# Which queue loads which half of the weights, and the order of the preparations in the first units of an FFT and maxout kernel

## The chip, the core and the metric

The kernel runs on one core of one Trainium2 chip. The metric is the device time of one execution in microseconds, the median over several runs. A kernel's profile is taken in an execution of its own and shows the span from its first to its last instruction. The engines are called TensorE (PE; PEld for its weight loads), VectorE (DVE), ScalarE (ACT), GpSimd (POOL) and SyncE (SP). DMAs that POOL issues go over the software queue, those of SP and ACT over hardware queues.

## The reference

For x of shape (8, 3072, 256): the real part of a two-dimensional Fourier transform over sequence and features, seen as 24576 rows of 256, and on it a maxout network with one output layer.

```python
X = np.fft.fft(np.fft.fft(x, axis=1), axis=2).real      # 8 x 3072 x 256
x = X.reshape(24576, 256)
h = np.maximum(np.maximum(x @ w1, x @ w2), x @ w3)      # 24576 x 768
out = h @ w_out                                         # 24576 x 256
```

w1, w2 and w3 are 256 x 768, w_out is 768 x 256, all float32.

## The kernel before

**The arithmetic.** The transform over the sequence is done in two stages, a transform of length 24 (the s steps, `s_half` and `s` in `Mix`) and one of length 128 with a table of sines (the k steps, `Mix.k`, and `Mix.end`). The s steps fill `z` (copied by `s_out`, L566), the k steps fill `t`, with its even part tE and odd part tO (copied by ACT at L610). The transform over the features is not done on x at all: its matrix `md` is multiplied into the weights. Since the maximum of three products is `x @ w1 + max(0, x @ (w2 - w1), x @ (w3 - w1))`, the kernel needs the differences d2 = w2 - w1 and d3 = w3 - w1 (`differences`, L231), then the products of md with them (`prep_first`, L481) and of md, w1 and w_out (`prep_second`, L506).

**The preparations.** `prep_first(jh, bank)` treats one half of the 768 columns (jh is 0 or 1): two pairs of matmuls for d3, two for d2, in four steps. After each step DVE copies the result to `gE` (L495), or ACT to `gO` (L497); `gD`, written by DVE at L501, is the product times the factor `dif`, which is derived from `sgn`. `gE`, `gO` and `gD` are written once per half; index 0 belongs to d2, index 1 to d3. `prep_second` has three g1t steps (md times w1, L513; the copies at L517 go to ACT for the first and to DVE for the other two), then psw (g1t times w_out, twelve matmuls at L523, copied to `gw` at L528) and the step `twice` (L531).

**The units.** The main loop (L938) goes over 8 batches, each of 3 blocks of 512 columns, each of 6 units jc of 128 of the 768 columns: 144 units in all. Unit jc makes four matmuls in two banks (`unit_plus`, L620: t times gE and gO), called plus here; ACT reads one bank with Relu into `stmp` (L640), DVE takes the maximum with the other bank into `hp` (L641). Then come the two matmuls of `unit_minus` with gD for the unit before (minus), and ACT and DVE read the same banks a second time, into `hm`. Each of the two banks of a unit has two buffers, so unit n needs the second reading of unit n - 2. After that `plan` runs what is planned for this unit (L978): in batch 0, units 0 to 9, the remaining preparations, k steps 2 to 5, the last sine tables (`tab_sines`, ACT), and the work of POOL that lays out batch 1's x. Units 0 to 2 use the first half of gE, gO and gD, units 3 to 5 the second.

**The order.** Everything is scheduled by hand: each engine executes its instructions in the order in which the program calls them, and waits for the semaphores of others. Tiles come from pools with a fixed number of buffers. The pool `ps_f` has two banks of PSUM; the k steps, the g1t steps, psw and `twice` take turns in them.

**The start.** POOL first issues twelve loads of batch 0's x (three groups of rows in four parts, L261), then three loads of weights (L268 to L270). SP issues the rest (L271 to L274), held back by a dependence on the first part of the last group of x (`last_part[0]`), and behind them the x rows of batch 1 (L463). A load of a half moves 256 x 384 numbers; w1 is converted to bf16 on the way, w2 and w3 arrive in float32 in `raw_w`. POOL then computes `sgn` and `dif` (L465 to L470), fills a few constants (L471 to L475; the last, `mark`, waits for DVE's copies of x, `laid`), makes the d3 difference of the first half and computes row numbers (`store_rows`, L276). DVE makes the d2 difference of the first half (L826); POOL both of the second half (L827), and issues the load of w_out (L828).

Of the kernel before, what the change touches and what calls it, by code (L numbers as in the profile page):

```python
# [13 lines left out]
ALU = mybir.AluOpType  # L14

ROUND = 12582912.0
AFTER = mybir.DependencyInfo(mybir.DependencyClass.Sync, mybir.DependencyReason.DATA)
# [16 lines left out]
def kernel(  # L34
# [9 lines left out]
    nc = tc.nc  # L44
# [39 lines left out]
    gw = consts.tile([128, 896], BF16, tag="gw")  # L84
    rows_m = consts.tile([128, 12 * B], INT32, tag="rows_m")
    mark = consts.tile([1, 1], FP32, tag="mark")
    two_row = consts.tile([128, 128], BF16, tag="two_row")
# [7 lines left out]
    sgn = consts.tile([128, 1], FP32, tag="sgn")  # L95
    dif = consts.tile([128, 1], FP32, tag="dif")
# [129 lines left out]
    raw_w = [consts.tile([128, 2 * DFF], FP32, name=f"raw_w{i}", tag=f"raw_w{i}") for i in (2, 3)]  # L226
# [4 lines left out]
    def differences(eng, jh, which=(0, 1), after=None):  # L231
        for i in which:
            done = eng.tensor_tensor(out=cols((d2_bf, d3_bf)[i], jh), in0=cols(raw_w[i], jh),  # L233
                                     in1=cols(w1_bf, jh), op=ALU.subtract)
            if after is not None:
                tc.add_manual_dep(done.ins, after.ins.name, AFTER, reason="the two share a port")
        return done

    whole = consts.tile([128, 64], FP32, tag="whole")
    rows_f, pidx, late = whole[:, 0:7 * B], whole[:, 56:57], whole[:, 57:58]  # L240
# [19 lines left out]
    for (r0, r1) in ((0, 40), (40, 84), (84, 112)):  # L260
        last_part = load_rows(nc.gpsimd, x0v[:, r0:r1, :], 0, r0, r1)  # L261

    def load_w(eng, wdst, wsrc, jh):
        return eng.dma_start(
            out=cols(wdst, jh),
            in_=wsrc.rearrange("(fc p) j -> p fc j", fc=2)[:, :, jh * 384:(jh + 1) * 384])

    load_w(nc.gpsimd, w1_bf, moe_w1, 0)  # L268
    load_w(nc.gpsimd, raw_w[1], moe_w3, 0)
    load_w(nc.gpsimd, w1_bf, moe_w1, 1)  # L270
    for (wsrc, wdst, jh) in ((moe_w2, raw_w[0], 0), (moe_w3, raw_w[1], 1),  # L271
                             (moe_w2, raw_w[0], 1)):
        ld = load_w(nc.sync, wdst, wsrc, jh)
        tc.add_manual_dep(ld.ins, last_part[0].ins.name, AFTER, reason="x first")  # L274

    def store_rows():  # L276
        rows_v = rows_f.rearrange("p (b r) -> p b r", r=7)
        iota(rows_v[:, :, 0:5], [[S // 2, B], [-1, 5]], base=S // 2 - 1, cm=-12)
        iota(rows_v[:, :, 5], [[S, B]], base=S - 11, cm=-24)
        iota(rows_v[:, :, 6], [[S, B]], base=S, cm=-24)  # L280
        nc.gpsimd.tensor_scalar(out=late, in0=pidx, scalar1=64.0, scalar2=float(S // 2 - 12),
                                op0=ALU.is_ge, op1=ALU.mult)
        nc.gpsimd.tensor_scalar(out=rows_v[:, :, 6], in0=rows_v[:, :, 6], scalar1=late,
                                scalar2=None, op0=ALU.add)
        iota(rows_v[0:1, :, 6], [[S, B]])
        nc.gpsimd.tensor_copy(rows_m[:, 0:7 * B], rows_f)
# [3 lines left out]
    for (name, value) in (("rnd", ROUND), ("n24", -24.0)):  # L290
# [10 lines left out]
                            op0=ALU.mult, op1=ALU.mult)  # L301
# [5 lines left out]
                                   op0=ALU.add, op1=ALU.subtract)  # L307
# [21 lines left out]
    def tab_sines(r0, r1, parts=(0, 1, 2)):  # L329
        wf = rows_of(r0, r1)  # L330
        wr = wf.rearrange("p (r j) -> p r j", j=128)
        if 0 in parts:
            nc.scalar.activation(out=tabs[:, r0:r1, 0, :], in_=wr, func=AX.Sin, scale=-turn)
        if 1 in parts:
            nc.scalar.activation(out=wf, in_=wf, func=AX.Abs)
        if 2 in parts:
            nc.scalar.activation(out=tabs[:, r0:r1, 1, :], in_=wr, func=AX.Sin, scale=-turn,
                                 bias=half_pi[:, 0:1])
# [5 lines left out]
    for (r0, r1) in ((0, 3), (3, 7)):  # L344
# [7 lines left out]
                            op0=ALU.mult)  # L352
# [8 lines left out]
                            op0=ALU.is_le)  # L361
# [4 lines left out]
                            op0=ALU.mult)  # L366
    nc.vector.tensor_scalar(out=six[:, 1:2], in0=ind24[:, 2:3], scalar1=-6.0, scalar2=None,
                            op0=ALU.mult)
    amp = gen.tile([96, 2], FP32, tag="amp")
    nc.vector.tensor_scalar(out=amp[:, 0:1], in0=ind24[:, 2:3], scalar1=ind24[:, 0:1],  # L370
                            scalar2=0.5, op0=ALU.add, op1=ALU.mult)
    nc.vector.tensor_scalar(out=amp[:, 1:2], in0=ind24[:, 2:3], scalar1=0.5, scalar2=None,
                            op0=ALU.mult)
# [7 lines left out]
    for (c0, c1, by) in ((0, 13, 1), (13, 24, 0), (24, 48, 0)):  # L381
        nc.vector.tensor_scalar(out=v24[:, 48 + c0:48 + c1], in0=v24[:, c0:c1],
                                scalar1=six[:, by:by + 1], scalar2=None, op0=ALU.add)
# [3 lines left out]
    for (m, c, by) in ((m24f, 0, ind24), (m24r, 24, ind24[:, ::-1])):  # L387
        nc.vector.tensor_tensor(
            out=m.rearrange("p (g r) -> p g r", g=4),
# [20 lines left out]
    def turn_rows(copy, r0, n, d0, d1):  # L410
        return reverse(copy, xr0, x0_first[:, r0 * 64:(r0 + n) * 64], r0, n, d0, d1)
# [9 lines left out]
    def bf_rows(r0, n):  # L421
# [19 lines left out]
    nc.vector.scalar_tensor_tensor(out=vm, in0=qm, scalar=-256.0 * ROUND, in1=vm,  # L441
                                   op0=ALU.add, op1=ALU.subtract)
    nc.scalar.activation(out=md[0], in_=vm, func=AX.Sin, scale=float(-2.0 * math.pi / 256.0))
    turn_rows(on_dve, 39, 44, 32, 65)
    lay_rows(on_act, bf_rows(40, 44), 40, 44, 12, 33)
    lay_rows(on_dve, bf_rows(40, 44), 40, 44, 0, 12)
# [15 lines left out]

    for ch in range(4):  # L463
        raw[1, ch] = load_chunk(1, ch)
    nc.gpsimd.tensor_scalar(out=sgn, in0=pidx, scalar1=0.0, scalar2=None,  # L465
                            op0=ALU.is_equal)
    nc.gpsimd.tensor_scalar(out=sgn, in0=sgn, scalar1=2.0, scalar2=-1.0,
                            op0=ALU.mult, op1=ALU.add)
    nc.gpsimd.tensor_scalar(out=dif, in0=sgn, scalar1=1.0, scalar2=None,
                            op0=ALU.subtract)  # L470
    nc.gpsimd.memset(two_row, 0.0)  # L471
    nc.gpsimd.memset(two_row[0:1], 2.0)
    nc.gpsimd.memset(gw[:, 512:513], 0.0)
    nc.gpsimd.memset(gw[0:1, 512:513], 1.0)
    first_op = nc.gpsimd.memset(mark, 0.0)  # L475
    tc.add_manual_dep(first_op.ins, laid.ins.name, AFTER, reason="the two share a port")

# [336 lines left out]
    m = Mix(0)  # L814
# [5 lines left out]
    for k in range(7):  # L820
        m.s_half(k, later, banks_s[k])
        m.s_out(k, banks_s[k], nc.vector.tensor_copy if k % 2 else nc.scalar.copy)
        if k == 1:
            differences(nc.gpsimd, 0, (1,))
            store_rows()
    first_half = differences(nc.vector, 0, (0,))  # L826
    differences(nc.gpsimd, 1, (1, 0), after=first_half)  # L827
    nc.gpsimd.dma_start(out=wout_bf.rearrange("p (jc c) -> p jc c", jc=NJC),  # L828
# [71 lines left out]
            pass  # L900
        l2_odd(0, 0)

    for (u, fn) in ((0, prep_some), (0, prep_some), (0, lambda: tab_sines(7, 10, (2,))),
                    (1, prep_some), (1, prep_some), (1, prep_some),
                    (2, lambda: m.k(2)), (2, prep_some), (2, lambda: tab_sines(10, 13, (0,))),
                    (3, prep_some), (3, lambda: tab_sines(10, 13, (1, 2))),
                    (4, lambda: m.k(3)), (4, prep_some), (5, prep_some), (5, l2_first),
                    (6, lambda: m.k(4)), (7, lambda: m.k(5)), (7, m.end),
                    (0, lambda: turn_chunk(1, 0)), (2, lambda: tab_minus(10, 13, nc.gpsimd)),
                    (2, lambda: turn_chunk(1, 1)),  # L910
                    (5, lambda: turn_chunk(1, 2)),
                    (7, lambda: turn_last(0)), (8, lambda: turn_last(1)),
                    (8, lambda: lay_last(0)), (9, lambda: lay_last(1)), (20, signed)):
        at(0, u, fn)
# [101 lines left out]
```

## Time and profile before

| | us |
|---|---|
| median of 3 runs | 406.31 (405.14 to 406.63) |
| profiled execution | 405.96 |
| its span | 404.1 |
| PE busy in the span | 387.6 |
| DVE busy | 308.2 |
| POOL busy | 298.1 |
| ACT busy | 265.2 |

PE is the busiest engine, with 96% of the span. The chain of work that ended last is PE's own for 92% of the span, DMA's for 4%, POOL's for 2%. Before the first unit lies the start, in which x is loaded, turned and sent through the s steps; PE's first matmuls, at 9.67, only multiply a table (`warm_up`). A timeline row reads: start, length, engine, line and operation, what is written and read, partitions and elements, the count of merged instructions, and in brackets the idle time of the engine ahead of it with what ended it. Matmuls are pipelined: the next one starts before the length given for the one before is over, so their starts, not their lengths, tell how long PE is occupied.

### The profile page before, as it was taken

Reading aid. Unit: us, or ns where it says so; the run is one execution under the profiler, and the core shown is the slowest. Engines: PE = TensorE matmul, PEld = TensorE weight load, DVE = VectorE, ACT = ScalarE, POOL = GpSimd, SP = SyncE. Lnnn points to the kernel's source line nnn. Section 1 sums busy time; section 2 is a strip of 40 time slices with the busy share of each in tenths; the row PEclk is TensorE's granted clock in tenths of the full one; section 3 lists DMA queues with packets and bytes.
Section 4 is the critical chain, followed back from the end, with each engine's and each line's share of the span. In section 5 each row is a group of like instructions: output and inputs, shape, how many; then the busy total and the mean of one; then the engine's idle time right before and its main releaser. Section 6 shows DMA issues by size and latency. Waiting matters only on the chain.

```text
span 404.1 us, 8723 instructions
## 1 busy us (share of the span) xinstructions
PE 387.6 (96%) x2936; PEld 260.0 (64%) x2936; DVE 308.2 (76%) x553; ACT 265.2 (66%) x488; POOL 298.1 (74%) x399
## 2 busy tenths in 40 slices
PE   0889999999999999999999999999999999999996
PEld 0445677766676666666666666766667677666665
DVE  8788776778777876687776887787777877678883
ACT  6878767656767567656776677666766676655550
POOL 9989989879987898679967898768967524323521
PEclk9999999999999999999999999999999999999999
DMA  9979897699878847796579728886234412211214
GB/s 114 185 180 171 172 241 201 162 216 195 190 183 207 192 131 180 198 214 170 131 201 232 163 72 226 213 174 177 74 110 118 118 55 78 80 54 53 106 54 157
DMA packets 127438, 62.08 MB, mean 154 GB/s; under 512 B 111616, under 2 KB 116496, under 8 KB 126816
## 3 DMA queue, kind: packets, MB, share of 16 engines
q1 hardware_dynamic: 101704, 41.82, 41.6%
q0 software_dynamic: 24752, 19.37, 24.5%
q8 instruction: 23, 0.38, 0.4%
q10 hardware_dynamic: 936, 0.33, 0.3%
q14 instruction: 23, 0.19, 0.2%
HBM read 33.74 MB, written 29.88 MB: 157 GB/s over the span
## 4 chain that ended last, share of the span: by engine, by line
PE 92%; DMA 4%; POOL 2%; DVE 1%; issue 0%; ACT 0%; SPq 0%; POOLq 0%; ACTq 0%
PE po L651 31%; PE pse L626 15%; PE pse L634 15%; PE pse L627 15%; PE ps L561 3%; PE po L675 3%; PE ps L608 3%; PE ps L606 3%; PE pl L664 2%; DMA raw_w<-in_moe_w_dram 2%; POOL x L111 2%; DMA x<-in_x_dram 2%; DVE hm L641 1%; POOL d_bf L233 0%; PE psw L523 0%
## 5 line engine op out<-in xcount | busy, mean ns | idle before, releaser
L640 ACT ACTIVATE stmp<-pse 128x512 bf16<-128x512 f32 x288 | 170.8, 600 | 53.6 <-PE pse L627 34.9
L641 DVE TENSOR_TENSOR hp<-pse,stmp 128x512 bf16<-128x512 f32 x144 | 99.6, 691 | 80.8 <-ACT stmp L640 52.9
L681 POOL TENSOR_TENSOR even<-even,other 128x256 f32<-128x256 f32 x92 | 70.3, 765 | 74.0 <-DVE other L678 73.7
L626 PE MATMUL pse<-t,gE 128*128 128x512 bf16 x288 | 109.2, 379 | 0.7 <-DVE gE L495 0.3
L627 PE MATMUL pse<-t,gO 128*128 128x512 bf16 x288 | 109.0, 378 | 0.0
L641 DVE TENSOR_TENSOR hm<-pse,stmp 128x512 bf16<-128x512 f32 x144 | 99.2, 689 | 3.4 <-ACT stmp L640 3.1
L651 PE MATMUL po<-wout_bf,hp 128*128 128x256 bf16 x576 | 85.9, 272 | 0.0
L634 PE MATMUL pse<-t,gD 128*128 128x512 bf16 x288 | 85.6, 379 | 0.0
L651 PE MATMUL po<-wout_bf,hm 128*128 128x256 bf16 x570 | 85.3, 273 | 0.0
L712 POOL DMA_INDIRECT out_dram<-ot,rows_m x53 | 54.1, 1021 | 20.5 <-DVE ot L705 12.5
L651 PEld LDWEIGHTS <-hp 128*128 128x128 bf16 x576 | 56.3, 98 | 17.3 <-issue 2.5
L651 PEld LDWEIGHTS <-hm 128*128 128x128 bf16 x576 | 56.3, 98 | 16.6
L705 DVE TENSOR_TENSOR ot<-po,even 128x512 f32<-128x512 f32 x92 | 62.8, 682 | 0.0
L173 POOL CAST xw<-xs 96x544 bf16<-96x544 f32 (+1 forms) x48 | 53.4, 1123 | 0.0
L178 POOL CAST xb<-xs 96x512 bf16<-96x512 f32 x48 | 52.5, 1101 | 0.0
L610 ACT CAST t<-ps 128x512 bf16<-128x512 f32 x48 | 27.9, 586 | 34.9 <-PE ps L608 34.8
L634 PEld LDWEIGHTS <-gD 128*128 128x128 bf16 x288 | 28.1, 98 | 32.3
L678 DVE SCALAR_TENSOR_TENSOR other<-twice,po 128x256 f32<-128x256 f32 x92 | 43.8, 476 | 0.1
L627 PEld LDWEIGHTS <-gO 128*128 128x128 bf16 x288 | 28.1, 98 | 20.3 <-issue 2.0
L626 PEld LDWEIGHTS <-gE 128*128 128x128 bf16 x288 | 28.2, 98 | 20.0 <-DVE gE L495 0.7
L570 ACT CAST z_all<-ps 128x480 bf16<-128x480 f32 x45 | 24.2, 561 | 21.6 <-PE ps L561 20.5
L667 ACT COPY even<-pl 128x512 f32<-128x512 f32 x46 | 27.0, 588 | 9.5 <-PE pl L664 8.1
(178 smaller groups left out, 373.9 us busy)
## 6 DMA issues: line engine op xcount, KB each, us to landing
xs<-in_x_dram SPq DMA_DIRECT2D x84, 198.0 KB
out_dram<-ot SPq DMA_DIRECT2D x39, 256.0 KB
xs<-in_x_dram SPq DMA_DIRECT2D x28, 192.0 KB
held<-xb SPq DMA_DIRECT2D x48, 96.0 KB
xw<-held POOLq DMA_DIRECT2D x24, 192.0 KB
out_dram<-ot SPq DMA_DIRECT2D x12, 128.0 KB
raw_w<-in_moe_w_dram SPq DMA_DIRECT2D x3, 384.0 KB
out_dram<-ot,rows_m POOLq DMA_INDIRECT x53
```

The costliest lines, as they stand in the source:

```text
L173: nc.gpsimd.tensor_copy(v[:, d0:d1, ch * 32:ch * 32 + 32], xs[:, 0:32 * 64].rearrange("p (bb dl) -> p dl bb", dl=64)[:, d0:d1, :])
L178: nc.gpsimd.tensor_copy(mir[:, d0:d1, c0:c0 + 32], bass.AP(xs.tensor, xs.offset + 33 * 64 - 1 - d0, [xs.ap[0], [-1, d1 - d0], [-64, 32]]))
L626: nc.tensor.matmul(pse[:, 0:n], gE[i][:, js], te, start=True, stop=False)
L627: nc.tensor.matmul(pse[:, 0:n], gO[i][:, js], to, start=False, stop=True)
L634: nc.tensor.matmul(pse, gD[i][:, js], to, start=False, stop=True, skip_group_check=True)
L640: nc.scalar.activation(out=stmp[:, 0:n], in_=pses[0][:, 0:n], func=AX.Relu)
L641: nc.vector.tensor_tensor(out=dst, in0=src3, in1=stmp[:, 0:n], op=ALU.max)
L651: nc.tensor.matmul(po, hcols(jc), wout_bf[:, jc * 256:(jc + 1) * 256], start=False, stop=(jc == NJC - 1), skip_group_check=True)
L678: nc.vector.scalar_tensor_tensor(out=other, in0=twice, scalar=po[:, 256:257], in1=po[:, 0:256], op0=ALU.mult, op1=ALU.subtract)
L681: nc.gpsimd.tensor_tensor(out=line[:, 256:512], in0=line[:, 0:256], in1=other, op=ALU.add)
L705: nc.vector.tensor_tensor(out=parts, in0=po.rearrange("p (i c) -> p i c", i=2), in1=lin.rearrange("p (i c) -> p i c", i=2), op=ALU.add)
L712: stored(nc.gpsimd.indirect_dma_start(out.rearrange("(n two) c -> n (two c)", two=2) if pair else out, bass.IndirectOffsetOnAxis(ap=rows_m ...
```

## The change

Three things are changed.

The loads: the first half of w2 goes over to POOL's queue, ahead of w1's second half. SP keeps the second halves of w3 and w2, and now waits for the last part of x (`last_part[3]`).

`sgn` and `dif` are computed on DVE, behind the preparation of `md`, no longer on POOL. The four memsets of `two_row` and of the last column of `gw` move on POOL from before the d3 difference of the first half to behind `store_rows`.

The plan of units 0 to 5: k step 2 goes from unit 2 to unit 0; the four steps of `prep_first(1)` go from units 0, 0, 1, 1 to units 1, 1, 2, 2; the three g1t steps from units 1, 2, 3 to units 3, 3, 4; in unit 4 there are now the third g1t step, k step 3 and psw, in this order. `twice` stays in unit 5.

```diff
     load_w(nc.gpsimd, w1_bf, moe_w1, 0)
     load_w(nc.gpsimd, raw_w[1], moe_w3, 0)
+    load_w(nc.gpsimd, raw_w[0], moe_w2, 0)
     load_w(nc.gpsimd, w1_bf, moe_w1, 1)
-    for (wsrc, wdst, jh) in ((moe_w2, raw_w[0], 0), (moe_w3, raw_w[1], 1),
-                             (moe_w2, raw_w[0], 1)):
-        ld = load_w(nc.sync, wdst, wsrc, jh)
-        tc.add_manual_dep(ld.ins, last_part[0].ins.name, AFTER, reason="x first")
+    for (wsrc, wdst) in ((moe_w3, raw_w[1]), (moe_w2, raw_w[0])):
+        ld = load_w(nc.sync, wdst, wsrc, 1)
+        tc.add_manual_dep(ld.ins, last_part[3].ins.name, AFTER, reason="x first")
...
     nc.scalar.activation(out=md[0], in_=vm, func=AX.Sin, scale=float(-2.0 * math.pi / 256.0))
+    nc.vector.tensor_scalar(out=sgn, in0=pidx, scalar1=0.0, scalar2=None,
+                            op0=ALU.is_equal)
+    nc.vector.tensor_scalar(out=sgn, in0=sgn, scalar1=2.0, scalar2=-1.0,
+                            op0=ALU.mult, op1=ALU.add)
+    nc.vector.tensor_scalar(out=dif, in0=sgn, scalar1=1.0, scalar2=None,
+                            op0=ALU.subtract)
     turn_rows(on_dve, 39, 44, 32, 65)
...
-    nc.gpsimd.tensor_scalar(out=sgn, in0=pidx, scalar1=0.0, scalar2=None,
-                            op0=ALU.is_equal)
-    nc.gpsimd.tensor_scalar(out=sgn, in0=sgn, scalar1=2.0, scalar2=-1.0,
-                            op0=ALU.mult, op1=ALU.add)
-    nc.gpsimd.tensor_scalar(out=dif, in0=sgn, scalar1=1.0, scalar2=None,
-                            op0=ALU.subtract)
-    nc.gpsimd.memset(two_row, 0.0)
-    nc.gpsimd.memset(two_row[0:1], 2.0)
-    nc.gpsimd.memset(gw[:, 512:513], 0.0)
-    nc.gpsimd.memset(gw[0:1, 512:513], 1.0)
     first_op = nc.gpsimd.memset(mark, 0.0)
...
             store_rows()
+            nc.gpsimd.memset(two_row, 0.0)
+            nc.gpsimd.memset(two_row[0:1], 2.0)
+            nc.gpsimd.memset(gw[:, 512:513], 0.0)
+            nc.gpsimd.memset(gw[0:1, 512:513], 1.0)
...
-    for (u, fn) in ((0, prep_some), (0, prep_some), (0, lambda: tab_sines(7, 10, (2,))),
-                    (1, prep_some), (1, prep_some), (1, prep_some),
-                    (2, lambda: m.k(2)), (2, prep_some), (2, lambda: tab_sines(10, 13, (0,))),
-                    (3, prep_some), (3, lambda: tab_sines(10, 13, (1, 2))),
-                    (4, lambda: m.k(3)), (4, prep_some), (5, prep_some), (5, l2_first),
+    for (u, fn) in ((0, lambda: tab_sines(7, 10, (2,))), (0, lambda: m.k(2)),
+                    (1, prep_some), (1, prep_some), (2, prep_some), (2, prep_some),
+                    (2, lambda: tab_sines(10, 13, (0,))),
+                    (3, prep_some), (3, prep_some), (3, lambda: tab_sines(10, 13, (1, 2))),
+                    (4, prep_some), (4, lambda: m.k(3)), (4, prep_some),
+                    (5, prep_some), (5, l2_first),
```

## The prediction

> **What bounds the kernel now.** I read the split by stretches first, then the timelines of the first 40 us engine by engine. In the stretches the columns after the length are busy us (and instructions) of PE, PEld, DVE, ACT and POOL, then the granted clock, DMA share and GB/s.
> ```profile
> span 404.1 us, 8723 instructions
> ...
> 21.00:40.00 19.00, 17.28 (x100) 9.69 (x99) 15.39 (x27) 14.39 (x30) 17.56 (x19) 1.00 0.84 170
> 40.00:396.00 356.00, 355.85 (x2644) 240.78 (x2643) 273.45 (x463) 234.91 (x433) 261.18 (x351) 1.00 0.60 152
> ```
> From 40 to 396 us PE is busy 355.85 of 356.00, so whatever moves the first units moves the end one for one. The change touches only what lies before 40. There PE waits, and the rows of POOL and SP say for what (start, length, in brackets the idle time before):
> ```profile
> 13.85 0.76 POOL L264 DMA_DIRECT2D raw_w<-in_moe_w_dram  x1
> 15.02 0.71 POOL L264 DMA_DIRECT2D w_bf<-in_moe_w_dram  x1 [0.41 <-DMA x<-in_x_dram]
> 15.76 1.11 POOL L465 TENSOR_SCALAR sgn<-whole 128x1 f32<-128x1 f32 x1
> ...
> 18.23 0.20 POOL L471 MEMSET two_row<- 128x128 bf16 x1
> ...
> 19.16 1.64 POOL L233 TENSOR_TENSOR d_bf<-raw_w,w_bf 128x768 bf16<-128x768 f32 x1
> ...
> 22.26 1.02 POOL L286 CAST rows_m<-whole 128x56 int32<-128x56 f32 x1
> 24.21 3.24 POOL L233 TENSOR_TENSOR d_bf<-raw_w,w_bf 128x768 bf16<-128x768 f32 x2 [0.93 <-DMA raw_w<-in_moe_w_dram]
> 27.39 0.94 POOL L828 DMA_DIRECT2D wout_bf<-in_moe_w_out_dram  x1
> ...
> 32.66 2.05 POOL L158 CAST x<-xs 96x1056 bf16<-96x1056 f32 x1
> ```
> ```profile
> 15.78 1.44 SPq L264 DMA_DIRECT2D raw_w<-in_moe_w_dram  x3
> 17.26 25.16 SPq L111 DMA_DIRECT2D xs<-in_x_dram  x16
> ```
> The second halves of the weights let POOL begin only at 24.21. On DVE the first half of w2 is late as well, by 0.56 at 22.23:
> ```profile
> 15.32 1.52 DVE L144 COPY back<-x 96x1452 bf16<-96x1452 bf16 x1 [0.85 <-DMA x<-in_x_dram]
> ...
> 18.15 0.70 DVE L417 COPY nat<-x 96x588 bf16<-96x588 bf16 x1
> 19.88 1.79 DVE L570 CAST z_all<-ps 128x480 bf16<-128x480 f32 x3 [1.03 <-PE ps L588]
> 22.23 0.96 DVE L233 TENSOR_TENSOR d_bf<-raw_w,w_bf 128x768 bf16<-128x768 f32 x1 [0.56 <-DMA raw_w<-in_moe_w_dram]
> ...
> 28.87 0.68 DVE L641 TENSOR_TENSOR hm<-pse,stmp 128x512 bf16<-128x512 f32 x1
> 29.47 0.55 DVE L495 CAST gE<-psg 128x384 bf16<-128x384 f32 x1
> 29.93 0.61 DVE L501 TENSOR_SCALAR gD<-psg,dif 128x384 bf16<-128x384 f32 x1
> ...
> 31.69 0.68 DVE L517 CAST g1t<-pst 128x512 bf16<-128x512 f32 x1
> ```
> PE's own rows are the yardstick: the first matmul of units 0 to 5 stands at 24.40, 26.55, 28.93, 31.34, 33.32 and 36.65.
> ```profile
> 24.40 0.39 PE L626 MATMUL pse<-t,gE 128*128 128x512 bf16 x1 [0.33 <-DVE gE L495]
> ...
> 25.06 0.38 PE L627 MATMUL pse<-t,gO 128*128 128x512 bf16 x1
> 25.90 0.81 PE L490 MATMUL psg<-d_bf,md_all 128*128 128x384 bf16 x4 [0.47 <-POOL d_bf L233]
> 26.55 0.38 PE L626 MATMUL pse<-t,gE 128*128 128x512 bf16 x1
> ...
> 28.93 0.38 PE L626 MATMUL pse<-t,gE 128*128 128x512 bf16 x1
> ...
> 29.60 0.38 PE L626 MATMUL pse<-t,gE 128*128 128x512 bf16 x1
> ...
> 31.34 0.38 PE L626 MATMUL pse<-t,gE 128*128 128x512 bf16 x1
> ...
> 33.32 0.38 PE L626 MATMUL pse<-t,gE 128*128 128x512 bf16 x1
> ...
> 34.04 0.38 PE L626 MATMUL pse<-t,gE 128*128 128x512 bf16 x1
> ...
> 35.34 1.47 PE L523 MATMUL psw<-wout_bf,g1t 128*128 128x256 bf16 x12
> 36.65 0.38 PE L626 MATMUL pse<-t,gE 128*128 128x512 bf16 x1
> ```
> Starts lie 0.22 apart for 512 columns (three steps from 24.40 to 25.06), 0.163 for 384 (four from 25.90 to 26.55), 0.11 for 256 (twelve from 35.34 to 36.65). What exceeds this between 24.40 and 36.65 is PE waiting: 0.62 before 25.90, 0.24 before 29.60, 0.24 from 31.34 to 33.32 (six steps of 512 and four of 256 fill 1.74 of it), 0.29 before 34.04: 1.39 in all.
>
> **The change, part by part.**
>
> *First halves.* That of w2 leaves SP's queue for POOL's, where it is issued at 15.02, in the place of w1's second half. The nearest price is w3's first half, issued on the same queue at 13.85 and in use at 19.16: at most 5.3 us. So w2 lands by about 20.3 (estimate); the other bound is its present landing, just before 22.23. DVE is held by its z copies until 19.88 + 1.79 = 21.67 in either case. I take 20.3, since the issue stands on the same queue 1.2 us behind: DVE starts 0.56 earlier, and so does unit 0, at 23.84.
>
> *Second halves.* w1's is issued about 15.8 instead of 15.02. SP's two loads now wait for the last part of x, not for the first of its group; that part is in use on ACT at 17.12, so the wait of 15.78 becomes at most 17.1.
> ```profile
> 17.12 0.80 ACT L144 COPY back<-x 96x261 bf16<-96x261 bf16 x2
> ```
> Behind it on SP stand the second batch's x rows (17.26); POOL first reads them at 32.66, and one load fewer is ahead of them: no cost. For the weights themselves there are two loads to move on SP instead of three, 1.3 us later. POOL can take them only at about 24.1 anyway: its rows last to 23.28, and the four memsets moved behind them add about 0.85 (18.23 to 19.09 now). I take 24.1, next to today's 24.21. PE asks for the result only at 26.5 (below), and POOL gives it at 24.1 + 1.64 = 25.74; a landing after 24.9 would cost us for us. wout's load follows at 27.3, not 27.39, and psw, which needs it, comes later than now: no cost.
>
> *sgn and dif on DVE.* Three 128x1 operations; DVE is idle for 0.85 before 15.32, and that wait for x hides them. Without it they cost at most that idle time. On POOL their going could start the difference of 19.16 up to 0.2 earlier, since DVE's copies, which it waits for, end at 18.85. PE can't use that: k step 0 behind it waits for z at 21.67.
>
> *The other order.* This is the large term. ACT's pieces, each of which starts about 0.1 before the one ahead has ended (two stmp in 1.07):
> ```profile
> 27.13 0.62 ACT L337 ACTIVATE tab<-w_late,half_pi 128x384 bf16<-128x384 f32 x1
> 27.64 1.07 ACT L640 ACTIVATE stmp<-pse 128x512 bf16<-128x512 f32 x2
> ...
> 31.10 0.59 ACT L610 CAST t<-ps 128x512 bf16<-128x512 f32 x1
> ```
> Unit 0 runs from 23.84 to 24.71. k step 2 (0.44) fills the hole in which PE waited for POOL, and unit 1 starts at 25.15, 1.40 ahead of 26.55. Minus 0 waits 0.07 for DVE, the d3 pair runs from 26.5, PE is free at 27.16.
> Unit 2 needs ACT to have read unit 0's sums a second time. ACT now has the sines (0.62) and the t copy (0.59) before that: stmp at 24.91, sines 25.41, t 25.94, stmp 26.44, stmp 26.93 to 27.53. PE starts at 27.57 (0.41 lost), and unit 2's second half waits for DVE's hm of unit 0, done at 28.37: 28.41 (0.41 lost).
> The d2 pair comes after minus 1, from 29.27 to 29.92. Unit 3 needs gE from it. DVE works in order: gE and gD of d3 (0.55, 0.61), hp of unit 2, then hm of unit 1, whose stmp can start only after minus 1 (29.27 to 29.87). So hm runs from 29.92 to 30.61 and gE ends at 31.08. Unit 3 starts at 31.12: 1.19 lost. Today that copy stands at 29.47, a unit before its use.
> Unit 3, minus 2 and two g1t steps (0.88) bring unit 4 to 33.30, level with 33.32. It loses 0.06; minus 3, the third g1t step and k step 3 end at 35.53, and psw stands directly behind both. In the built program psw has the bank that k step 3 used, so it waits for ACT's t copy, which comes after two stmp: 35.74 to 36.33, psw at 36.37 (0.84 lost). Its fifth matmul reads the third g1t, which DVE copies behind hp 4 and hm 3: 37.18 (0.41 lost). Eight more matmuls: unit 5 at 38.10.
> Waiting is now 0.07 + 0.41 + 0.41 + 1.19 + 0.06 + 0.84 + 0.41 = 3.39 against 1.39: +2.00. With unit 0 earlier by 0.56: **+1.44 us**, a span of 405.5. The profiled execution took 405.96 with its span of 404.1, which is 0.35 under the median of the runs, 406.31; added to that median: **407.7**.
>
> A rule speaks against moving w2 to POOL. POOL's issues of x take (min/median/max, ns):
> ```profile
> L111 POOL DMA_DIRECT2D x<-in_x_dram x12: 777/930/1746, 1.5 to 12.3; - x12
> ```
> The Trainium skill, SBUF — State Buffer, section "SBUF: two separate sides", says that GpSimd can't write a DMA's descriptors while VectorE runs certain copies, and that a hardware queue is free of this. The 1746 would fit it; the issue at 15.02, beside DVE's copy of 15.32, took 0.71 and doesn't. By the row the sum is the one above, by the rule the far end of the next case.
>
> **Rivals.** *Late weights (slower).* The place is DVE's difference of w2; it decides once w2 lands after 21.57, and from there each us costs one. If the software queue brings it no sooner than SP's does now, so that the change doesn't do what it says, DVE starts at 22.23 again and +2.00 is left: 408.3. If DVE's copies, which end at 18.85, hold POOL's issue until then, w2 lands at 18.85 + 5.3 = 24.15, DVE starts 2.0 later than now: +4.0, 410.3. For: the 1746. Against: 0.71 at 15.02.
> *The new waits are covered.* The losses at unit 3 and psw rest on the order within DVE and ACT. If they sum to no more than today's 1.39, only -0.56 is left: 405.8. For: DVE is busy 15.39 and ACT 14.39 of 19.00 us. Against: the queues run in order, so idle time elsewhere is no help.
> *All waits go.* Then the 1.39 fall away too: -1.95, 404.4. Only unit 1's early start speaks for it.
>
> **How the numbers follow.** Forecast 0.57 (own range 407.0 to 408.5), late weights 0.25 (408.3 to 410.3; 0.07 of it the held issue), covered waits 0.13 (405.2 to 406.5), all gone 0.05 (403.9 to 404.8). The range leaves out the top of the late weights, the bottom of the covered waits and the last: 405.6 to 409.4. 0.5% of 406.31, about what a measurement of this kernel can tell from no change, is 2.03, so the bounds are 404.28 and 408.34. Faster: over half of the last case, 0.03. Slower: 0.08 of the forecast and 0.23 of the late weights, 0.31. Same: 0.66.
>
> **What would show it.** Right: DVE's difference of w2 at about 21.7 without a wait for its load; unit 1 over 1 us earlier than 26.55; PE idle for about 1.2 us before unit 3, put down to gE on DVE; psw interrupted after four matmuls; unit 5 near 38.1; 40 to 396 as full as now. Wrong: unit 5 at or before 36.65, DVE waiting for raw_w beyond 22.2, or POOL's second differences after 24.9.

## The result and the profile after

The changed kernel is slower by about 0.4%: the ratio to the kernel before is 1.0044, 95% interval 1.0027 to 1.0061, over 17 runs of each. On the median before in this series, 405.26 us, that is +1.78 us (1.09 to 2.47). The median after is 406.81, 1.55 above it. The forecast was +1.44. Its 407.7 lies higher than the measured time because it was put on the first three runs of before, whose median of 406.31 is 1.05 above that of the seventeen.

The head of the page after and its split by stretches (columns as before: busy us and instructions of PE, PEld, DVE, ACT and POOL, granted clock, DMA share, GB/s):

```profile
span 404.6 us, 8724 instructions
...
21.00:40.00 19.00, 16.27 (x93) 8.98 (x93) 13.86 (x24) 13.17 (x27) 17.99 (x20) 1.00 0.80 161
40.00:396.00 356.00, 355.80 (x2640) 240.62 (x2640) 273.23 (x464) 235.31 (x435) 259.79 (x350) 1.00 0.60 152
```

From 40 us on PE is as full as it was: 355.80 of 356.00 against 355.85. Between 21 and 40 PE is busy for 16.27 us instead of 17.28. PE's timeline after, from the last matmul of the s steps to the first of unit 5:

```profile
19.84 0.21 PE L584 MATMUL ps<-m24r,back 96*64 96x96 bf16 x1
...
23.11 0.39 PE L622 MATMUL pse<-t,gE 128*128 128x512 bf16 x1 [0.33 <-DVE gE L491]
...
24.43 0.38 PE L622 MATMUL pse<-t,gE 128*128 128x512 bf16 x1
...
26.94 0.38 PE L622 MATMUL pse<-t,gE 128*128 128x512 bf16 x1 [0.21 <-ACT stmp L636]
...
27.77 0.38 PE L622 MATMUL pse<-t,gE 128*128 128x512 bf16 x1 [0.24 <-DVE hm L637]
...
30.46 0.39 PE L622 MATMUL pse<-t,gE 128*128 128x512 bf16 x1 [1.01 <-DVE gE L491]
...
32.64 0.38 PE L622 MATMUL pse<-t,gE 128*128 128x512 bf16 x1
...
33.34 0.38 PE L622 MATMUL pse<-t,gE 128*128 128x512 bf16 x1
...
35.91 1.64 PE L519 MATMUL psw<-wout_bf,g1t 128*128 128x256 bf16 x12 [0.67 <-ACT t L606]
37.40 0.38 PE L622 MATMUL pse<-t,gE 128*128 128x512 bf16 x1
```

In the profiled execution of before, the same last matmul of the s steps stands 0.74 later:

```profile
20.58 0.21 PE L588 MATMUL ps<-m24r,back 96*64 96x96 bf16 x1
```

So the two executions are compared from that point on. From it to unit 0 it is 3.27 us now and 3.82 before; from unit 0 to unit 5 14.29 and 12.25; from unit 5 to the end of the span 367.20 and 367.45. With -0.74 these make -0.74 - 0.55 + 2.04 - 0.25 = +0.50, the difference of the spans. The work that PE does between unit 0 and unit 5 is the same in both, 12.25 - 1.39 = 10.86, so PE now waits 3.43 us there instead of 1.39. The s steps' end differs by 0.74 between these two executions, so the runs, and not the two spans, tell what the change costs.

### The profile page after: what moved, and what is told of

It is laid out like the page before. It is cut to its first block, busy times and chain, and to the rows that moved or that the text cites. A ratio compares the mean times of both kernels' runs of the same rounds, so it can differ in the third digit from the quotient of the medians.

```text
span 404.6 us, 8724 instructions
## 1 busy us (share of the span) xinstructions
PE 387.7 (96%) x2936; PEld 259.8 (64%) x2936; DVE 308.1 (76%) x556; ACT 264.5 (65%) x488; POOL 295.7 (73%) x397
## 4 chain that ended last, share of the span: by engine, by line
PE 89%; POOL 4%; DMA 3%; ACT 1%; issue 1%; DVE 1%; SPq 0%; POOLq 0%; ACTq 0%
PE po L647 30%; PE pse L622 15%; PE pse L630 15%; PE pse L623 15%; PE po L671 3%; PE ps L557 3%; POOL x L111 3%; PE ps L604 2%; PE ps L602 2%; PE pl L660 2%; DMA raw_w<-in_moe_w_dram 2%; DMA x<-in_x_dram 1%; DVE hm L637 1%; PE psw L519 0%; POOL d_bf L233 0%
```

## The experiments

All were measured against the kernel before in runs of the same chip; a ratio is the time over that of before, with its 95% interval. "Unit 0 to 5" is read from PE's timeline of each run's profile, as above. Short diffs are against the changed kernel unless said otherwise.

**The loads alone.** The changed kernel with the plan of before.

```diff
-    for (u, fn) in ((0, lambda: tab_sines(7, 10, (2,))), (0, lambda: m.k(2)),
-                    (1, prep_some), (1, prep_some), (2, prep_some), (2, prep_some),
...
+    for (u, fn) in ((0, prep_some), (0, prep_some), (0, lambda: tab_sines(7, 10, (2,))),
+                    (1, prep_some), (1, prep_some), (1, prep_some),
...
```

> All of the change but the order: loads, sgn and dif on DVE and the moved memsets as in the changed kernel, units 0 to 4 in the order of before. Theory (the new order costs +2.00, the loads gain 0.56 at unit 0): DVE takes w2's difference straight behind its z copies; PE then waits about 0.8 us instead of 0.62 before the d3 pair of the second halves, because POOL's difference ends at about the same place as now while PE comes earlier; unit 0 to unit 5 takes about 12.4 us (12.25 before, 14.29 in the changed kernel), and the time is 0.4 us below before, ratio 0.999. Rival (the loads are what costs, by later second halves): unit 0 to unit 5 takes over 13.5 us, ratio 1.003 to 1.005.

Ratio 1.0013 (0.9993 to 1.0032): no difference that can be told, and the theory's 0.999 lies outside. Unit 0 to 5 took 35.89 - 23.15 = 12.74, nearer to the theory's 12.4 than to the rival's 13.5, but 0.49 more than in before. PE's rows and one of ACT:

```profile
23.15 0.82 PE L622 MATMUL pse<-t,gE 128*128 128x512 bf16 x2 [0.33 <-DVE gE L491]
24.85 0.81 PE L486 MATMUL psg<-d_bf,md_all 128*128 128x384 bf16 x4 [0.66 <-POOL d_bf L233]
...
32.44 0.38 PE L622 MATMUL pse<-t,gE 128*128 128x512 bf16 x1 [0.23 <-ACT stmp L636]
33.28 0.38 PE L622 MATMUL pse<-t,gE 128*128 128x512 bf16 x1 [0.24 <-DVE hm L637]
...
35.89 0.38 PE L622 MATMUL pse<-t,gE 128*128 128x512 bf16 x1
```

```profile
30.90 0.52 ACT L333 ACTIVATE tab<-w_late 128x384 bf16<-128x384 f32 x1 [0.27 <-POOL w_late L327]
```

Unit 0 came 3.28 after the s steps, 0.54 earlier than in before, and nearly all of that is waited for again: for POOL's difference of the second half before 24.85 (0.82 by the distance of starts, 0.62 in before), and at unit 4, where ACT's reading stands behind sines that wait for POOL's angles.

**The order alone.** The kernel before with the new plan.

> Only the order of units 0 to 4, with the loads, sgn, dif and memsets of before. Theory: unit 0 starts as in before, with the 0.5 us wait of DVE for w2; unit 0 to unit 5 takes 14.2 to 14.3 us against 12.25, PE waits about 1.1 us before unit 3 for gE on DVE, and about 0.8 us before psw for ACT's t copy; ratio 1.005, 0.5 us above the changed kernel. Rival (the order is neutral, the loads cost): 12.3 us, ratio within 1.001 of before.

Ratio 1.0051 (1.0036 to 1.0067). Unit 5's first record is missing in this trace; its second matmul stands at 38.12, so that it began about 0.22 earlier, at 37.90, 14.28 after unit 0. PE's rows:

```profile
23.62 0.82 PE L626 MATMUL pse<-t,gE 128*128 128x512 bf16 x2 [0.33 <-DVE gE L495]
...
30.97 0.39 PE L626 MATMUL pse<-t,gE 128*128 128x512 bf16 x1 [1.01 <-DVE gE L495]
...
36.20 0.60 PE L523 MATMUL psw<-wout_bf,g1t 128*128 128x256 bf16 x4 [0.67 <-ACT t L610]
37.02 1.05 PE L523 MATMUL psw<-wout_bf,g1t 128*128 128x256 bf16 x8 [0.22 <-DVE g1t L517]
```

The order makes the whole loss. The sum of the waits is that of the changed kernel to 0.01 us; only its parts differ, 0.05 at unit 4's second half and 0.38 before psw's fifth matmul here, 0.27 and 0.17 there. DVE's wait for w2, with the old loads, was smaller here than in before's profile, 0.21 instead of 0.56 (DVE's row):

```profile
21.46 0.96 DVE L233 TENSOR_TENSOR d_bf<-raw_w,w_bf 128x768 bf16<-128x768 f32 x1 [0.21 <-DMA raw_w<-in_moe_w_dram]
```

**w2's first half back on SP's queue.**

```diff
-    load_w(nc.gpsimd, raw_w[0], moe_w2, 0)
...
-    for (wsrc, wdst) in ((moe_w3, raw_w[1]), (moe_w2, raw_w[0])):
-        ld = load_w(nc.sync, wdst, wsrc, 1)
+    for (wsrc, wdst, jh) in ((moe_w2, raw_w[0], 0), (moe_w3, raw_w[1], 1),
+                             (moe_w2, raw_w[0], 1)):
+        ld = load_w(nc.sync, wdst, wsrc, jh)
```

> The changed kernel with w2's first half back on SP's queue, ahead of the two second halves, all three behind the last part of x. Theory: w2 lands 1 to 2 us later than in the changed kernel, DVE's difference waits for it by 0.5 us or more, and the whole delay stays: unit 0 and unit 5 are later by the same 0.5 to 1.0 us, ratio 1.0055 to 1.007 to before. Rival (a chain that doesn't begin with w2, through POOL's angles, ACT and the third g1t, sets psw): unit 0 is later, unit 5 is not, ratio 1.0045 as the changed kernel.

Unit 0 to 5 took 15.69 us in the trace (unit 5's first record is missing here and in the next trace too, and its start is reckoned as above). The ratio, 1.0051 (1.0033 to 1.0070), can't be told from the changed kernel's 1.0044. Both theories missed the place. The rows of DVE and of POOL: DVE did not wait for w2 at all, and unit 0 came 3.28 after the s steps, as in the changed kernel; POOL waited for the loads behind w2 on SP.

```profile
20.95 0.95 DVE L233 TENSOR_TENSOR d_bf<-raw_w,w_bf 128x768 bf16<-128x768 f32 x1
```

```profile
25.17 3.25 POOL L233 TENSOR_TENSOR d_bf<-raw_w,w_bf 128x768 bf16<-128x768 f32 x2 [1.97 <-DMA raw_w<-in_moe_w_dram]
```

POOL's lateness went on, through its angles and ACT's sines, to 1.12 us of idle time at unit 4. In the changed kernel the first of these two differences starts 2 us earlier, without a wait; but in the next run, which has the loads of the changed kernel, it waits as well (one row of each):

```profile
23.12 1.65 POOL L233 TENSOR_TENSOR d_bf<-raw_w,w_bf 128x768 bf16<-128x768 f32 x1
```

```profile
24.68 3.24 POOL L233 TENSOR_TENSOR d_bf<-raw_w,w_bf 128x768 bf16<-128x768 f32 x2 [1.23 <-DMA raw_w<-in_moe_w_dram]
```

So this pair of profiles doesn't show that w2's leaving SP is what brings w3's second half early. It does show an execution in which DVE had no wait for w2 that the move could have saved.

**The d2 pair one unit earlier**, straight behind the d3 pair.

```diff
-                    (1, prep_some), (1, prep_some), (2, prep_some), (2, prep_some),
+                    (1, prep_some), (1, prep_some), (1, prep_some), (1, prep_some),
```

> The changed kernel with the d2 pair of the second halves moved up from unit 2 to unit 1, straight behind the d3 pair. Theory: the 1.01 us before unit 3 (gE on DVE) goes to under 0.3, but not for nothing: the d2 pair comes to PE at about 26.5, where POOL's difference of w2 ends at 26.8 and DVE has not yet emptied the two banks of the d3 pair, so that unit 2 starts 0.5 to 2 us later than now; unit 5 is no earlier, 0 to 0.8 us later, ratio 1.004 to 1.0065. Rival (the place of the pair alone makes the wait): unit 3 and unit 5 come 1.0 earlier, ratio 1.002.

Ratio 1.0059 (1.0044 to 1.0075), unit 0 to 5 15.11. As the theory had it, the wait moved: the pair itself now waits for DVE to empty the d3 pair's banks, and unit 3 waits less. Part of it has a second reason: POOL's difference for the pair, the second of the two in this run's row above, ended only at 27.92. PE's rows:

```profile
28.61 1.00 PE L486 MATMUL psg<-d_bf,md_all 128*128 128x384 bf16 x4 [1.42 <-DVE gE L491]
...
31.38 0.38 PE L622 MATMUL pse<-t,gE 128*128 128x512 bf16 x1 [0.47 <-ACT stmp L636]
```

**The third g1t step in unit 3**, so that unit 4 has k step 3 and psw alone.

```diff
-                    (3, prep_some), (3, prep_some), (3, lambda: tab_sines(10, 13, (1, 2))),
-                    (4, prep_some), (4, lambda: m.k(3)), (4, prep_some),
+                    (3, prep_some), (3, prep_some), (3, prep_some), (3, lambda: tab_sines(10, 13, (1, 2))),
+                    (4, lambda: m.k(3)), (4, prep_some),
```

> The changed kernel with the third g1t step moved from unit 4 up to unit 3, so that unit 4 holds k step 3 and psw alone. Theory (psw waits because k step 3 and the third g1t stand right ahead of it): its waits of 0.84 and 0.16 us go, a new one of about 0.4 before the third g1t step (its bank waits for ACT's copy of the first) comes in; unit 0 to unit 5 takes 13.6 us instead of 14.29, ratio 1.0025 to 1.003. Rival (the delay at unit 3 comes through to psw by another chain): psw still waits about 1 us, 14.2 to 14.3 us, ratio 1.0044.

Ratio 1.0013 (0.9999 to 1.0027), unit 0 to 5 13.41: the largest gain of one edit, and the theory's place. The waits of 0.84 and 0.17 are gone. psw starts at 35.23, 0.12 behind the last matmul of k step 3, before ACT can have copied that step, so it no longer has the same bank. The new wait of 0.40 is there, ahead of the third g1t step. PE's rows:

```profile
33.06 0.60 PE L509 MATMUL pst<-md_all,w_bf 128*128 128x256 bf16 x4 [0.24 <-ACT g1t L513]
...
35.23 1.49 PE L519 MATMUL psw<-wout_bf,g1t 128*128 128x256 bf16 x12
36.55 0.38 PE L622 MATMUL pse<-t,gE 128*128 128x512 bf16 x1
```

**One copy of gE moved from DVE to ACT**, the one for which unit 3 waits.

```diff
-                    nc.vector.tensor_copy(out=gE[i][:, cs], in_=psg[:, 0:384])
+                    (nc.vector.tensor_copy if i or not jh else nc.scalar.copy)(
+                        out=gE[i][:, cs], in_=psg[:, 0:384])
```

> The changed kernel with one copy moved from DVE to ACT: gE of the d2 pair's second half, for which PE waits 1.18 us before unit 3. Theory (DVE's order, hp of unit 2 and hm of unit 1 ahead of that copy, makes the wait): the wait falls to about 0.1, 0.4 come back at gO, which now stands behind gE on ACT; unit 3 is 0.7 us earlier, and if the waits add up unit 5 as well: 13.6 us from unit 0, ratio 1.0027. Rival (waits do not add up, what is gained at unit 3 is waited at psw): unit 3 0.7 earlier, unit 5 within 0.2 of the changed kernel, ratio 1.004.

Unit 3 comes 6.58 after unit 0 instead of 7.35, unit 5 13.68 instead of 14.29: DVE's order is the cause of that wait, and 0.61 of the 0.77 comes through in the trace, as the theory had it. The wait before unit 3 goes from 1.18 to 0.41, not to 0.1. PE's row:

```profile
31.54 0.39 PE L623 MATMUL pse<-t,gE 128*128 128x512 bf16 x1 [0.25 <-ACT gE L491]
```

The interval of the ratio, 1.0039 (1.0024 to 1.0054), is too wide to tell the two theories apart.

**The sines of rows 7 to 9 from unit 0 to unit 3.**

```diff
-    for (u, fn) in ((0, lambda: tab_sines(7, 10, (2,))), (0, lambda: m.k(2)),
+    for (u, fn) in ((0, lambda: m.k(2)),
...
-                    (3, prep_some), (3, prep_some), (3, lambda: tab_sines(10, 13, (1, 2))),
+                    (3, prep_some), (3, prep_some), (3, lambda: tab_sines(7, 10, (2,))), (3, lambda: tab_sines(10, 13, (1, 2))),
```

> The changed kernel with the sines of rows 7 to 9 (0.62 us of ACT) moved from unit 0 to unit 3. Theory that the terms add up: the first wait of unit 2 (0.37 us, ACT behind the sines) goes, units 2 to 4 and unit 5 are 0.4 us earlier, ratio 1.0035. Rival (psw is the end of a chain on ACT, and the sines only change their place on it): units 2 to 4 are 0.4 earlier, psw waits 0.3 to 0.5 longer for the t copy, unit 5 stays within 0.1 of 14.29 us after unit 0, ratio 1.0044.

The trace fits the rival; the ratio, 1.0043 (1.0028 to 1.0058), can't tell its 1.0044 from the theory's 1.0035. In this execution the granted clock was low ahead of unit 0 (more of that in the last section); from unit 0 on the starts of the matmuls lie 0.22 apart as elsewhere. Unit 2 comes 0.39 and unit 4 0.51 earlier after unit 0 (3.44 and 9.02 against 3.83 and 9.53), and unit 5 stays at 14.29 to the hundredth, because psw waits 1.20 for the t copy and 0.52 for the third g1t. That last copy starts 12.67 after unit 0, as in the changed kernel (35.78 there): the moved sines stand on ACT ahead of unit 4's stmp, for which DVE waits. PE's rows and one of DVE:

```profile
26.95 0.39 PE L622 MATMUL pse<-t,gE 128*128 128x512 bf16 x1 [0.29 <-DVE gE L491]
...
35.97 0.38 PE L622 MATMUL pse<-t,gE 128*128 128x512 bf16 x1
...
39.39 0.60 PE L519 MATMUL psw<-wout_bf,g1t 128*128 128x256 bf16 x4 [1.03 <-ACT t L606]
40.35 1.05 PE L519 MATMUL psw<-wout_bf,g1t 128*128 128x256 bf16 x8 [0.37 <-DVE g1t L513]
41.24 0.38 PE L622 MATMUL pse<-t,gE 128*128 128x512 bf16 x1
```

```profile
39.62 0.68 DVE L513 CAST g1t<-pst 128x512 bf16<-128x512 f32 x1
```

**Five attempts at a faster version.** They use these findings: the order of before with k step 3 in unit 3 and the last sines in unit 4. The texts put down before these runs call the s steps layer 1.

```diff
+    for (u, fn) in ((0, prep_some), (0, lambda: tab_sines(7, 10, (2,))), (0, prep_some),
+                    (1, prep_some), (1, prep_some), (1, prep_some),
+                    (2, lambda: m.k(2)), (2, prep_some), (2, lambda: tab_sines(10, 13, (0,))),
+                    (3, prep_some), (3, lambda: m.k(3)),
+                    (4, prep_some), (4, lambda: tab_sines(10, 13, (1, 2))),
+                    (5, prep_some), (5, l2_first),
```

The first also computes POOL's last angles on DVE, in its idle time before the z copies, and puts the memsets back in front.

```diff
+    tab_angles(10, 13)
     warm_up(1, third_turned)
...
-    tab_angles(10, 13, nc.gpsimd)
```

> A version put together from what the first runs show: the loads of the changed kernel, the four memsets back where they stood before, the angles of rows 10 to 12 on DVE (two operations of 0.56 us in its 1.06 us of waiting for PE ahead of the z copies) instead of POOL (3.0 us), and the order of before with k step 3 moved from unit 4 to unit 3 and the last sines to unit 4. Theory: POOL's second difference ends 0.7 us earlier than in the run with the loads alone, the 0.82 us before the d3 pair falls to under 0.2, ACT no longer waits for POOL's angles; unit 0 to unit 5 takes 11.3 to 11.8 us (12.25 in before, 12.74 with the loads alone), ratio 0.997 to 0.9985. Rival (the angles delay DVE's z copies, or the second halves land too late): over 12.3 us, ratio 0.9995 or more.

Ratio 0.9990 (0.9977 to 1.0003), unit 0 to 5 11.38, the shortest of all. The trace is where the theory had it; the ratio, outside the theory's range, has an interval that holds the theory's 0.9985 and the rival's 0.9995 alike. Unit 0 comes 3.52 after the s steps, 0.25 later than in the changed kernel. POOL's rows show by what: a memset takes up to 0.79 beside DVE's copies, and the first difference 1.97 instead of 1.65, ending at 21.12.

```profile
17.27 0.79 POOL L472 MEMSET two_row<- 1x128 bf16 x1
...
19.15 1.97 POOL L233 TENSOR_TENSOR d_bf<-raw_w,w_bf 128x768 bf16<-128x768 f32 x1 [0.42 <-DMA raw_w<-in_moe_w_dram]
```

The second has the four memsets behind w_out's load; the third adds k step 2 behind unit 0, with the first g1t step and the sines of rows 7 to 9 one unit later.

> The version of the last run with the four memsets neither in front (where they took 0.55 to 0.79 us each beside DVE's copies and held POOL's first difference to 21.1) nor between POOL's differences, but behind wout's load. Theory: POOL's first difference ends early enough that PE waits under 0.3 us for it instead of 0.74, so that unit 0 comes 3.3 us after the end of layer 1 instead of 3.52; unit 0 to unit 5 stays at 11.2 to 11.7 us; ratio 0.997 to 0.998. Rival (what unit 0 gains is waited for the second halves behind it, whose loads have not landed): unit 0 to unit 5 grows by the same, ratio 0.999.

> The same with k step 2 right behind unit 0, as the changed kernel has it, and the sines of rows 7 to 9 in unit 1. Theory (in the change it is not k step 2 that costs, but the d2 pair a unit later and k step 3 with the third g1t right ahead of psw): k step 2 fills PE's wait before the d3 pair, unit 0 to unit 5 is within 0.3 of the run without this step, 11.2 to 11.8 us, ratio 0.997 to 0.9985. Rival (k step 2's t copy on ACT pushes the stmp of unit 0 back and with it units 2 and 3): over 12.2 us, ratio 1.000 or more.

Ratios 1.0007 (0.9991 to 1.0022) and 0.9999 (0.9986 to 1.0011): no gain. Unit 0 to 5 took 11.39 and 11.62, so in this order k step 2 right behind unit 0 costs little, and it is not what costs in the change; but unit 0 came 4.45 and 4.57 after the s steps. The rows of DVE and of POOL in the version with the late memsets show why: POOL's difference now starts ahead of it, and DVE's second operation of the angles takes 1.89 instead of 0.56, with the z copies behind it.

```profile
18.77 1.89 DVE L322 SCALAR_TENSOR_TENSOR w_late<-w_late 128x384 f32<-128x384 f32 x1
20.59 1.77 DVE L566 CAST z_all<-ps 128x480 bf16<-128x480 f32 x3
```

```profile
18.60 1.65 POOL L233 TENSOR_TENSOR d_bf<-raw_w,w_bf 128x768 bf16<-128x768 f32 x1 [0.17 <-DMA raw_w<-in_moe_w_dram]
```

The fourth is the kernel before with the angles on DVE and this order; the fifth has the new loads, the angles on POOL, the memsets behind them, and w_out's load between POOL's two last differences.

> The loads, sgn, dif and memsets of before, with the angles of rows 10 to 12 on DVE and the order of the last two versions but one (k step 3 in unit 3, the last sines in unit 4). Theory (the change's loads bring the time about nothing, the order and the angles bring what is gained): unit 0 to unit 5 takes 11.3 to 12.0 us, ratio 0.997 to 0.9995, within 0.001 of the version with the new loads. Rival (the new loads gain 0.5 us or more at unit 0): ratio over 0.9995 and at least 0.0015 above the version with the new loads.

> The loads of the changed kernel with POOL's work in another order (no memsets ahead of the second differences but behind the angles, wout's load between the two differences), the angles of rows 10 to 12 on POOL again, and the order of before with k step 3 in unit 3 and the last sines in unit 4. Theory (the 1.9 us of the angles' second operation on DVE beside POOL's difference was the whole of the 1.56 us that PE waited before k step 0): DVE's z copies start without that delay, unit 0 comes 3.3 us after the end of layer 1, the second halves are waited for by 0.3 to 0.5 us twice, unit 0 to unit 5 takes 11.4 to 11.8 us; ratio 0.996 to 0.9985. Rival (an earlier unit 0 only waits longer for the second halves or for wout): unit 0 to unit 5 over 12.2 us, ratio 0.9995 or more.

The old loads gave 1.0008 (0.9992 to 1.0024) with 11.42 us from unit 0 to 5. That is level with the second version, of the same series, and 0.0018 above the first, of another series, more than the rival's 0.0015; the intervals overlap. So what the new loads are worth can't be told here either. The last gave 1.0008 (0.9984 to 1.0033) with 12.36 us: the rival's outcome. Unit 0 was back at 3.27 after the s steps, and PE waited 0.81 and 0.60 by the distance of starts for POOL's differences of the second halves. PE's rows:

```profile
25.21 0.81 PE L486 MATMUL psg<-d_bf,md_all 128*128 128x384 bf16 x4 [0.65 <-POOL d_bf L233]
...
27.75 0.81 PE L486 MATMUL psg<-d_bf,md_all 128*128 128x384 bf16 x4 [0.44 <-POOL d_bf L233]
```

In some of these executions the gain is given back later too. The rows of POOL and of PE in the run with the third g1t in unit 3: POOL waited for the second chunk of batch 1's x, and PE for a bank that DVE could empty only behind POOL.

```profile
39.00 2.01 POOL L158 CAST x<-xs 96x1056 bf16<-96x1056 f32 x1 [1.98 <-DMA xs<-in_x_dram]
```

```profile
49.09 0.27 PE L671 MATMUL po<-gw,t 128*128 128x257 bf16 x1 [0.91 <-DVE ot L701]
```

No version beats the kernel before by more than the measurement can tell.

## Why the prediction was right, point by point

The table sets the places that the prediction gave against the profile after; 0.74 is taken off, since the s steps ended that much earlier there than in the profile on which it was built.

| PE reaches | predicted, less 0.74 | measured |
|---|---|---|
| unit 0 | 23.10 | 23.11 |
| unit 1 | 24.41 | 24.43 |
| unit 2, its second half | 26.83, 27.67 | 26.94, 27.77 |
| unit 3 | 30.38 | 30.46 |
| unit 4 | 32.56 | 32.64 |
| psw | 35.63 | 35.91 |
| unit 5 | 37.36 | 37.40 |

From the last matmul of the s steps to unit 5 the trace after is 2.04 - 0.55 = 1.49 longer than before, where the forecast had 1.44.

*The order* was the large term, as forecast: 3.39 us of waiting predicted, 3.43 measured, with the causes that were named (unit 3 behind gE, psw behind ACT's t copy). The order alone and the loads alone split the change: 14.28 and 12.74 us, ratios 1.0051 and 1.0013. They don't add: the 0.49 that unit 0 to 5 grew by with the loads alone is not in the changed kernel's 14.29, where k step 2 fills the hole ahead of the d3 pair.

*Unit 3's wait* was put down to gE's place on DVE. DVE after:

```profile
28.63 0.68 DVE L637 TENSOR_TENSOR hp<-pse,stmp 128x512 bf16<-128x512 f32 x1
29.24 0.69 DVE L637 TENSOR_TENSOR hm<-pse,stmp 128x512 bf16<-128x512 f32 x1
29.85 0.55 DVE L491 CAST gE<-psg 128x384 bf16<-128x384 f32 x1
...
35.78 0.68 DVE L513 CAST g1t<-pst 128x512 bf16<-128x512 f32 x1
```

hp and hm stand ahead of it, as worked out; with the copy on ACT unit 3 came 0.77 earlier.

*psw's two waits* were sized 0.84 and 0.41. The first is 0.84; of the second only 0.17 is left (35.91 to 37.40 is 1.49 for 1.32 of work), because unit 4's second half had already lost 0.27 instead of 0.06. The fifth matmul can't start before the third g1t copy ends at 36.46, whatever was lost ahead of it. So the 0.84, though it is there, is not a price of its own: without it psw would have begun at 35.08 and stopped before its fifth matmul at 35.52, until the same 36.46 (an estimate from these rows; no run takes the t copy's wait away alone).

*The sum* of the waits came out because each was worked out with those ahead of it already in their places. Its terms are not prices that can be saved one by one. With gE's copy on ACT, 0.61 of the 0.77 saved at unit 3 came through to unit 5. With the late sines, nothing of the 0.39 to 0.51 saved at units 2 to 4 did, because ACT's queue got the same sines back ahead of psw: ACT's t copy and DVE's third g1t are ends of chains that run beside PE.

*w2's first half, -0.56.* Unit 0 came 0.55 earlier after the s steps than in the profile of before, but that this meets the forecast is in part luck. The term was sized from one execution. DVE's wait for w2 with the old loads was 0.56 in one profile and 0.21 in another; with w2 on SP behind the last part of x it was nil, and unit 0 stood at 3.28 all the same. The loads alone bring no time that can be told, and the interval of the result, 1.09 to 2.47, holds the order's +2.00 by itself as well as +1.44: the runs don't confirm this term. The second halves were taken to cost nothing, and in the profile of the changed kernel PE did not wait for them; but POOL waited for the first of them 0.93 in before, 1.97 with w2 on SP and 1.23 with the d2 pair early, and in the other profiles for no load at that place. What decides that is open.

*The rivals.* Late weights did not come: DVE's difference of w2 started at 20.84 without a wait, and unit 0 stands at 3.27 after the s steps. The waits were not covered. Of the 1.39 the 0.62 ahead of the d3 pair did go, as forecast, but the new ones are far larger.

*sgn and dif* took three operations of 0.15 on DVE, from 13.97 to 14.49, and the copy of x followed at 14.52 without a wait. No wait was left behind them, so it can't be told how much of them the wait for x hid; they cost at most 0.5, within the forecast's bound of 0.85. Whether the earlier end of the s steps in the profile after (19.84 against 20.58) has to do with them is open. With the old loads it stood at 20.58, 20.16 and 20.50 in three profiles, with the new ones between 19.84 and 20.40 in nine at full clock.

## What to carry to other kernels

Waits of an engine that is otherwise full need not add up over a change of order: work them out one behind the other, each engine's queue in order, and test a term by removing it, since what it saves can be waited for again at the next join. When a step is moved later, look at the in-order queue of the engine that copies its result, and at which buffer the next step gets. When a load is moved to another queue, look first in several executions whether it was waited for: the 0.56 of one profile was 0.21 in the next and nil in a third.

## What the runs showed of the hardware

*POOL's issue of a load is held by DVE's copy.* The forecast thought it not so, from an issue of 0.71 at 15.02. That issue began 0.30 before the copy and was over 0.41 into it. In the changed kernel the last issue falls into it (a row of DVE and one of POOL):

```profile
14.52 1.55 DVE L144 COPY back<-x 96x1452 bf16<-96x1452 bf16 x1
```

```profile
14.88 1.28 POOL L264 DMA_DIRECT2D w_bf<-in_moe_w_dram  x1
```

It ends at 16.16, 0.09 after the copy at 16.07. In the run with k step 2 first an issue went from 14.97 to 16.71, there that of w2's first half, and the copy from 15.18 to 16.63. So an issue that begins 0.21 before the copy is held, too. The Trainium skill, SBUF — State Buffer, section "SBUF: two separate sides", has GpSimd unable to write descriptors until VectorE lets go of the port pair that they share; these rows agree. It cost nothing here, since w1's second half was not what POOL waited for: its difference at 23.12 had no wait.

*Of DVE's second operation of the angles and POOL's difference, the later one waits.* DVE's operation of 0.56 took 1.89 when POOL's difference had begun 0.17 earlier, and ended 0.41 after it; with the memsets in front, DVE's operation had begun 0.10 earlier (19.05 against 19.15), kept its 0.56, and POOL's difference took 1.97 instead of 1.65. The same section of the Trainium skill calls the pair an exclusive lock held for the whole instruction, which fits both. It is not so for every operation: in the changed kernel DVE's z copies (19.14 to 20.92) lie beside POOL's difference (18.59 to 20.24), and neither is longer than elsewhere, 1.78 and 1.65.

*The clock.* In the profiled run with the late sines x came late, PE stood idle for 2.22 us between the table's matmuls and the s steps, and the granted clock fell to half (PE's first row of the s steps, and the stretch from 20 to 24 us with the columns as above):

```profile
17.79 0.23 PE L584 MATMUL ps<-m24f,nat 96*64 96x96 bf16 x1 [2.22 <-DVE nat L417]
```

```profile
20.00:24.00 4.00, 4.00 (x72) 3.20 (x69) 2.90 (x5) 2.07 (x6) 3.15 (x12) 0.50 1.09 294
```

The last matmul of the s steps stands at 22.29 instead of 19.84, and that execution took 410.27 us, the longest of its kernel's. With 1.87 us of idle time at the same place, in the run with gE on ACT, the clock of this stretch was 0.66; with 1.72, in the run with the old loads, and 1.55, in before, it stayed at 1.00. That the idle time is the cause was not tried.
